# Output projection of the last stage on two steps at once, in one written order

## The chip, the core and the metric

The kernel runs on one core of a Trainium2 chip. The metric is the time of one execution on the device in microseconds, median of a few runs. Five engines work side by side, each through its own queue of instructions in order: TensorE (PE, its weight loads shown apart as PEld), VectorE (DVE), ScalarE (ACT), GpSimd (POOL) and SyncE (SP), which here only issues transfers. An engine waits for another only where an instruction carries a wait.

## The reference

The inputs are x (2048 tokens of 640 numbers), weights in fp32, 32 heads of 20 numbers each. Two branches are computed and mixed by a gate per token:

```
g   = sigmoid(x . gate_w)
q, k, v = x @ wqkv, per head
phi(t) = [softmax(t @ w_phi), softmax(-(t @ w_phi))]        # 40 numbers a head
kv  = sum over tokens of phi(k)^T v ;  z = sum of phi(k)
o   = (phi(q) @ kv) / (phi(q) . z + 1e-6)
a   = o @ wo
b   = silu(x @ w1) @ w2
out = g * a + (1 - g) * b
```

## The kernel before

Everything is kept transposed on the chip: features on the 128 partitions, tokens along the free side. Nearly every product is made from a high part and a low part of each number (fp32r each), in three passes: high x high, high x low, low x high (`PASSES`). The keys and values come first, then branch b, whose result, already multiplied by 1 - g, is written to a buffer in device memory (`fb_d`). The last stage makes branch a for the 2048 tokens and adds `fb_d` to it. The change concerns only this stage.

The last stage goes by steps u = 0 to 7 of 256 tokens, that is two q tiles of 128 tokens each. The tiles of steps 0 and 1 are finished before it; those of steps 2 to 7 are numbered 0 to 11 here (`QT`), tiles 2u - 4 and 2u - 3 for step u. A q tile goes through this chain:

- projection (pq, `q_proj`, line 542): 30 matmuls of 320 columns on TensorE, from a split x (`xb_load`, `xb_split`: a transfer, a cast on ScalarE, a difference on POOL);
- spikes (`q_max`, `q_sub`, lines 526 to 533): maximum and minimum per head, and two differences, on VectorE;
- exponential (`q_exp`, line 1192) on ScalarE;
- sum (`q_sum`, line 1196) on VectorE, and beside it the product with z (`q_norm`, ez, line 1209) on POOL, whose sum (`q_norm_sum`, line 1212) is again VectorE's;
- small sums (`q_small`: lines 1223 to 1239) on VectorE, which give each head's factor, and its product with the exponentials (`q_mul`, line 1245) on POOL.

A step u then is:

- transposes (pT, `t_mm`, line 1480): six of them on TensorE, each copied out of PSUM by ScalarE to fT (`t_out`, line 1496);
- the heads' products (pn, `n_mm`, line 1587), in three parts; ScalarE casts each part's high half to oT (`n_hi`, lines 1600 to 1603) and VectorE makes the low half, the remainder (`n_lo`, lines 1608 and 1610);
- output projection (pa, `w_mm`, line 1629): for each of five blocks of 128 output features 16 matmuls of 256 columns: five chunks in each of the three passes, and a rest. The first ten need only high halves of oT, the next five the low halves, and the last the rest. Two blocks share one PSUM bank (groups 0, 2, with 32 matmuls), the fifth has its own (group 4, with 16).

Then the sum: in steps 0 to 4 ScalarE copies the group out of PSUM (`w_copy`, line 1641) and POOL adds it to y, which a transfer brought from `fb_d` (`w_add`, line 1647); in steps 5 to 7 VectorE adds it straight out of PSUM. A transfer stores y.

PSUM banks: projections of q have two pairs of banks (`pair`). All other tiles of this stage, pT, pn and pa, take four single banks in turn (`single`), so each tile waits until the tile four calls before has been read. 

What sets the order: within the stage the queues of TensorE, VectorE, ScalarE and POOL keep the order in which the functions are called (`inorder`); SyncE's order is set by a scheduler. `step(u)` runs the transposes of step u, the output projection of step u - 1, two projections, and the heads' products of step u, interleaved by hand; `last_steps` writes out the end.

Of the kernel before, what the change touches and what calls it, by code (L numbers as in the profile page):

```python
# [16 lines left out]
P = 128  # L17
# [32 lines left out]
PAB = 2  # L50
# [78 lines left out]
NSEV = 4  # L129
ORDERS = (HEAD, O1, O2, O3, O4, O5, O6, O7, O8, O9, O10)  # L130
# [4 lines left out]
def mix_kernel(ctx: ExitStack, tc: tile.TileContext, xT, wqT, wkc, wkr, wv, bd, bdc, cst, wo, w1, w1r, w2, out):  # L135
# [1439 lines left out]

    def n_mm(u, gp, a):
        if (gp, a) == (0, 0):
            oTs[u] = tb.tile([P, 2, NG + 1, 256], F32R, tag="oT", name=f"oT{u}", bufs=2)
# [16 lines left out]
    pns = {}  # L1595

    def n_hi(u, gp):
        o, pn = oTs[u], pns[u, gp]
        if gp < 2:
            nc.scalar.copy(o[:, 0, 2 * gp : 2 * gp + 2, :], pn)  # L1600
        else:
            nc.scalar.copy(o[:, 0, 4, :], pn[:, 0])
            nc.scalar.activation(o[:GW, 1, 5, :], pn[:GW, 1], AF.Copy, scale=stk[:GW, 0:1])

    def n_lo(u, gp):
        o, pn = oTs[u], pns.pop((u, gp))
        k = slice(2 * gp, 2 * gp + 2) if gp < 2 else slice(4, 5)
        nc.vector.tensor_tensor(o[:, 1, k, :], pn[:, : k.stop - k.start], o[:, 0, k, :].bitcast(F32), op=ALU.subtract)  # L1608
        if gp == 2:
            nc.vector.scalar_tensor_tensor(  # L1610
                o[:GW, 0, 5, :], pn[:GW, 1], stk[:GW, 1:2], o[:GW, 1, 5, :].bitcast(F32), op0=ALU.mult, op1=ALU.add
            )

    ws = {}

    def w_mm(u, m0, n):
        o = oTs[u]
        if m0 == 2:
            y = fu.tile([P, 512], F32, tag="ur", name=f"y{u}_{m0}", bufs=2).rearrange("p (a s) -> p a s", a=2)
        else:  # L1620
            y = tb.tile([P, 2, 256], F32, tag="y", name=f"y{u}_{m0}", bufs=2)
        cols = slice(PB[u] * 256, (PB[u] + 1) * 256)
        nc.sync.dma_start(y[:, :n], fb_d[m0 : m0 + n, :, cols].rearrange("m p s -> p m s"))
        pa = single(f"pa{u}_{m0}").rearrange("p (a s) -> p a s", a=2)
        todo = [(c, ho, hw) for ho, hw in PASSES for c in range(NG)] + [(NG, 0, 0)]
        for a in range(n):
            ds = slice((m0 + a) * P, (m0 + a + 1) * P)
            for k, (c, ho, hw) in enumerate(todo):
                nc.tensor.matmul(  # L1629
                    pa[:, a, :],  # L1630
                    wo_tile[0][:, c, hw, ds] if c < NG else WOR[:, ds],
                    o[:, ho, c, :] if c < NG else o[:GW, ho, c, :],
                    start=(k == 0),
                    stop=(k == len(todo) - 1),
                )
        ws[u, m0] = y, pa, n, cols

    def w_copy(u, m0):
        y, pa, n, cols = ws[u, m0]
        a = tb.tile([P, 2, 256], F32, tag="pa", name=f"pac{u}_{m0}", bufs=PAB)[:, :n]  # L1640
        nc.scalar.copy(a, pa[:, :n])
        ws[u, m0] = y, a, n, cols

    def w_add(u, m0):
        y, pa, n, cols = ws.pop((u, m0))
        eng = nc.vector if pa.space == PSUM else nc.gpsimd
        eng.tensor_tensor(y[:, :n], pa[:, :n], y[:, :n], op=ALU.add)
        nc.sync.dma_start(out[m0 * P : (m0 + n) * P, cols].rearrange("(m p) s -> p m s", p=P), y[:, :n])

    def on(t, *todo):  # L1650

        if 0 <= t < len(QT):
            for part in todo:
                part(QT[t])

    def q_mm(t):
        q_open(t, q_proj(t))

    def x_next(k):
        for p in range(xb_done[0], min(xb_done[0] + k, len(XP))):  # L1660
            xb_split(p)
            x_ahead(p + 4)
            xb_done[0] = p + 1

    def x_ahead(p):
        if p < len(XP):
            xb_load(p)

    xb_done = [3]
    for p in range(3, 5):  # L1670
        x_ahead(p)

    def t_all(u, first, last):
        for i in range(first, last):
            t_mm(u, i)
            t_out(u, i)

    def n_all(u):
        for gp in range(3):
            for a in range(2):  # L1680
                n_mm(u, gp, a)
            n_hi(u, gp)

    def spikes(t):
        on(t, q_max, lambda t: q_sub(t, 0), lambda t: q_sub(t, 1), q_exp)

    def step(u):
        a, b, c = 2 * u - 2, 2 * u - 1, 2 * u
        x_next(3)
        t_all(u, 0, 4)  # L1690
        on(b, q_mm)
        on(a, q_norm_sum)
        t_all(u, 4, 6)
        spikes(b)
        on(a, q_small)
        on(b, q_norm)
        on(a, q_mul)
        w_mm(u - 1, 0, 2)
        w_copy(u - 1, 0)
        w_add(u - 1, 0)  # L1700
# [132 lines left out]
```

## Time and profile before

| | |
|---|---|
| median of 3 runs | 730.0 us (729.78 to 730.61) |
| the profiled execution | 730.17 us |
| its span in the trace | 728.4 us |
| TensorE busy, matmuls / weight loads | 721.2 us / 621.0 us |
| VectorE, ScalarE, POOL busy | 429.9, 297.4, 395.6 us |

The span is what lies between the first and the last instruction; the execution takes a little more. A row of a group of instructions gives line, engine, operation, what is written from what, shape and count, then busy time, mean ns of one, and the idle time of the engine just ahead of them with what ended it. A row of the chain gives start, length, engine, tile, line and number of instructions merged. A row of the order of time has start and length in us and ends with the idle time ahead in brackets. Matmuls run into one another, so the spacing of a run of them, its length divided by its number, is their price, not the duration of one.

### The profile page before, as it was taken

How to read it: one execution, taken by the hardware profiler on the slowest of the kernel's cores; microseconds unless marked ns; L12 is line 12 of the kernel's file. 1: busy time of each engine (PE TensorE's matmuls, PEld its weight loads, DVE VectorE, ACT ScalarE, POOL GpSimd, SP SyncE). 2: the span in 40 equal slices, each digit the busy share in tenths (PEclk: the TensorE clock that was granted, in tenths of full speed). 3: DMA queues.
4: the chain of work that ended last, by engine and by line, in shares of the span. 5: the costliest groups of instructions: out<-in, count | busy, mean ns of one | idle time of the engine just before them, and what ended most of it. 6: DMA issues, size and time to landing. Idle time of an engine off the chain costs nothing.

```text
span 728.4 us, 12513 instructions
## 1 busy us (share of the span) xinstructions
PE 721.2 (99%) x4935; PEld 621.0 (85%) x4935; DVE 429.9 (59%) x708; ACT 297.4 (41%) x558; POOL 395.6 (54%) x307
## 2 busy tenths in 40 slices
PE   9999999999999999999999999999999999999998
PEld 8888888888888888888888788788997899999988
DVE  4565555565253557568525656653887766766652
ACT  5333322336466354435344323535334453435330
POOL 2354545534756475572766447311598867767440
PEclk9999999999999999999999999999999999999999
DMA  8111111114734577588965623342133332121222
GB/s 306 56 56 56 46 56 55 63 35 135 238 116 176 213 276 277 207 314 324 330 205 188 219 68 107 109 117 73 52 115 119 102 95 83 56 94 45 74 87 81
DMA packets 50751, 98.80 MB, mean 136 GB/s; under 512 B 6352, under 2 KB 25828, under 8 KB 50692
## 3 DMA queue, kind: packets, MB, share of 16 engines
q1 hardware_dynamic: 50692, 98.00, 40.0%
q8 instruction: 39, 0.64, 0.4%
q14 instruction: 20, 0.16, 0.1%
HBM read 66.15 MB, written 31.84 MB: 135 GB/s over the span
## 4 chain that ended last, share of the span: by engine, by line
PE 97%; DVE 1%; ACT 1%; DMA 1%; issue 0%; DVEq 0%; ACTq 0%
PE o L1053 18%; PE kvp L566 17%; PE pa L1629 10%; PE pq L542 9%; PE a L964 9%; PE o L1094 5%; PE ph L632 3%; PE c L964 3%; PE b L964 3%; PE d L964 3%; PE pn L1587 3%; PE pT L1480 2%; PE hp L651 2%; PE kvt L553 2%; PE o_m L1116 1%; PE kvp L440 1%
## 5 line engine op out<-in xcount | busy, mean ns | idle before, releaser
L1053 PE MATMUL o<-u,w 128*128 128x512 f32 x580 | 142.5, 391 | 0.0
L1053 PEld LDWEIGHTS o<-u,w 128*128 128x128 f32 x580 | 108.0, 188 | 22.7 <-DVE acc L1058 0.6
L566 PE MATMUL kvp<-wh,xa 128*128 128x480 f32 (+2 forms) x420 | 92.5, 360 | 0.0
L566 PEld LDWEIGHTS kvp<-wh,xa 128*128 128x128 f32 x420 | 72.8, 188 | 10.4
L1629 PE MATMUL pa<-oT,wo 128*128 128x256 f32 x600 | 77.1, 281 | 0.1
L363 POOL TENSOR_TENSOR w<-wr,w 128x640 fp32r<-128x640 f32 x26 | 41.8, 1615 | 64.5 <-ACT w L352 64.5
L1629 PEld LDWEIGHTS pa<-oT,wo 128*128 128x128 f32 x600 | 73.8, 188 | 1.1 <-DVE oT L1608 0.8
L1209 POOL TENSOR_TENSOR ez<-eq,zbc 128x1280 f32<-128x1280 f32 x16 | 48.0, 3002 | 47.6 <-DVE sm L1239 24.6
L594 POOL TENSOR_TENSOR ek<-ek,st 128x1280 f32<-128x1280 f32 x16 | 38.2, 2386 | 50.3 <-DVE st L593 42.1
L542 PE MATMUL pq<-wq,xb 128*128 128x320 f32 x360 | 55.9, 312 | 0.0
L542 PEld LDWEIGHTS pq<-wq,xb 128*128 128x128 f32 x360 | 52.9, 188 | 2.2 <-DVE oT L1608 2.0
L1058 DVE TENSOR_TENSOR acc<-acc,o 128x512 f32<-128x512 f32 x70 | 46.4, 679 | 14.2 <-PE o L1053 14.1
L978 ACT ACTIVATE v<-v 128x512 f32<-128x512 f32 x33 | 20.9, 632 | 82.9 <-DVE v L997 36.2
L194 POOL TENSOR_TENSOR xa<-xra,xa 128x512 fp32r<-128x512 f32 (+1 forms) x26 | 26.4, 1038 | 41.4 <-ACT xa L192 37.0
L566 PE MATMUL kvp<-wl,xa 128*128 128x480 f32 (+2 forms) x210 | 47.6, 356 | 0.0
L1192 ACT ACTIVATE eq<-eq 128x1280 f32<-128x1280 f32 x16 | 20.4, 1276 | 63.9 <-DVE eq L533 63.9
L980 DVE TENSOR_TENSOR u<-v,u 128x512 fp32r<-128x512 f32 x29 | 21.5, 742 | 34.4 <-ACT u L979 31.5
L399 ACT COPY v<-kvp 128x340 f32<-128x340 f32 (+1 forms) x30 | 12.5, 417 | 70.1 <-PE kvp L566 68.2
L566 PEld LDWEIGHTS kvp<-wl,xa 128*128 128x128 f32 x210 | 36.6, 188 | 4.8
L1084 DVE TENSOR_TENSOR acc<-acc,o 128x512 f32<-128x512 f32 x48 | 31.3, 682 | 15.6 <-PE o L1094 12.1
L1245 POOL TENSOR_TENSOR eq<-eq,sm 128x1280 f32<-128x1280 f32 x16 | 37.9, 2368 | 1.0 <-DVE sm L1239 0.8
L592 DVE TENSOR_REDUCE st<-ek 128x64 f32<-128x1280 f32 x16 | 23.8, 1487 | 22.7 <-ACT ek L728 21.3
(236 smaller groups left out, 1483.7 us busy)
## 6 DMA issues: line engine op xcount, KB each, us to landing
wr<-w SPq DMA_DIRECT2D x33, 320.0 KB
w_d<-w SPq DMA_DIRECT2D x15, 640.0 KB
xr<-xT SPq DMA_DIRECT2D x27, 256.0 KB
w<-w_d SPq DMA_DIRECT2D x10, 640.0 KB
fb_d<-acc SPq DMA_DIRECT2D x20, 256.0 KB
s_d<-s SPq DMA_DIRECT2D x8, 512.0 KB
sa<-s_d SPq DMA_DIRECT2D x8, 512.0 KB
y<-fb_d SPq DMA_DIRECT2D x16, 256.0 KB
```

The costliest lines, as they stand in the source:

```text
L363: eng.tensor_tensor(t[:, 1, :], r[:, :D], t[:, 0, :].bitcast(F32), op=ALU.subtract)
L542: nc.tensor.matmul(dst, xt[c][:, hx, :], w[:, c, hw, lo : lo + n], start=first, stop=(hx == 1 and c == NC - 1))
L566: nc.tensor.matmul(kv_cols(t, lo, hi), xt[c][:, hx, :], WKV[hw][:, c, w_cols(lo, hi)], start=(n == 0), stop=(n == 3 * NC - 1), skip_group_ ...
L594: nc.gpsimd.tensor_tensor(groups(e), groups(e), spread(st[:, 1, :]), op=ALU.mult)
L964: last["mm"] = nc.tensor.matmul(out, lhs, rhs, start=(first and i == 0), stop=(stop and i == len(todo) - 1), skip_group_check=True)
L1053: nc.tensor.matmul(o, lhs, rhs, start=(n == 0), stop=(n == len(todo) - 1))
L1058: nc.vector.tensor_tensor(acc[j][m], acc[j][m], o, op=ALU.add)
L1084: nc.vector.tensor_tensor(acc[j][m], acc[j][m], o, op=ALU.add)
L1094: nc.tensor.matmul(o, ws[hw], x()[hx], start=(first and i == 0), stop=(i == len(PASSES) - 1), skip_group_check=True)
L1209: nc.gpsimd.tensor_tensor(ez, Q[t]["e"], zbc, op=ALU.mult)
L1245: nc.gpsimd.tensor_tensor(groups(q["e"]), groups(q["e"]), spread(q["sm"][:, 2 * H : 4 * H]), op=ALU.mult)
L1629: nc.tensor.matmul(pa[:, a, :], wo_tile[0][:, c, hw, ds] if c < NG else WOR[:, ds], o[:, ho, c, :] if c < NG else o[:GW, ho, c, :], start= ...
```

## The change

Steps are put together in groups p for the output projection: (0, 1), (2, 3), (4, 5), 6 and 7. For the three pairs oT holds 512 columns, the two steps side by side, the rest has a tile of its own (oR, with its high half in oM), and each of the five blocks is one PSUM bank, 16 matmuls of 512 columns. Steps 6 and 7 keep 256 columns. `w_mm` can be called in two halves. All adds are VectorE's, out of PSUM; the copies to `pac` and their buffers are gone. The helper functions of the order (`step`, `last_steps` and others) are replaced by one list of names, `FIN`, of which this is the beginning:

```diff
-PAB = 2
+FIN = """
+t04 f04 t05 f05 q0p R n000 n001 h00 n010 n011 h01 n020 n021 h02 x5l x6l q0m l00 l01 l02 q0s0 q0s1 t10
...
+    OUT = ((0, 1), (2, 3), (4, 5), (6,), (7,))
...
     def n_mm(u, gp, a):
         if (gp, a) == (0, 0):
-            oTs[u] = tb.tile([P, 2, NG + 1, 256], F32R, tag="oT", name=f"oT{u}", bufs=2)
+            p = max(u // 2, u - 3)
+            k = OUT[p].index(u)
+            if k == 0:
+                oTs[p] = (
+                    tb.tile([P, 2, NG, 512], F32R, tag="oT", name=f"oT{p}", bufs=2),
+                    tb.tile([P, 512], F32R, tag="oR", name=f"oR{p}", bufs=2),
+                )
+            cols = slice(k * 256, (k + 1) * 256)
+            mids[u] = oTs[p][0][:, :, :, cols], oTs[p][1][:GW, cols]
...
+    def w_parts(p, m0):
+        n = 1 if p < 3 else min(2, NC - m0)
+        return n, 256 * len(OUT[p]), PB[OUT[p][0]] * 256
+
+    def w_mm(p, m0, k):
+        o, rest = oTs[p]
+        n, size, at = w_parts(p, m0)
+        if k == 0:
+            pool, tag = (fu, "ur") if m0 // (1 if p < 3 else 2) % 2 else (tb, "y")
+            y = pool.tile([P, 512], F32, tag=tag, name=f"y{p}_{m0}", bufs=2)[:, : n * size]
+            y = y.rearrange("p (a s) -> p a s", a=n)
+            nc.sync.dma_start(y, fb_d[m0 : m0 + n, :, at : at + size].rearrange("m p s -> p m s"))
+            ws[p, m0] = y, single(f"pa{p}_{m0}")[:, : n * size].rearrange("p (a s) -> p a s", a=n)
+        pa = ws[p, m0][1]
+        todo = [(a, i) for a in range(n) for i in range(len(TERMS))]
+        half = len(todo) // 2
+        for a, i in todo[half * k : half * (k + 1)]:
+            c, ho, hw = TERMS[i]
             ds = slice((m0 + a) * P, (m0 + a + 1) * P)
...
+            nc.tensor.matmul(
+                pa[:, a, :],
+                wo_tile[0][:, c, hw, ds] if c < NG else WOR[:, ds],
+                o[:, ho, c, :size] if c < NG else rest[:GW, :size],
+                start=(i == 0),
+                stop=(i == len(TERMS) - 1),
+            )
...
-    def w_copy(u, m0):
-        y, pa, n, cols = ws[u, m0]
-        a = tb.tile([P, 2, 256], F32, tag="pa", name=f"pac{u}_{m0}", bufs=PAB)[:, :n]
-        nc.scalar.copy(a, pa[:, :n])
-        ws[u, m0] = y, a, n, cols
...
+    def w_add(p, m0):
+        y, pa = ws.pop((p, m0))
+        n, size, at = w_parts(p, m0)
+        nc.vector.tensor_tensor(y, pa, y, op=ALU.add)
+        nc.sync.dma_start(out[m0 * P : (m0 + n) * P, at : at + size].rearrange("(m p) s -> p m s", p=P), y)
...
+        for name in FIN.split():
+            ops.pop(name)()
```

Three places show how instructions move. In the rows a number after a name is the step (pT, fT, pn), the group (oT, pa, y) and its block, or the tile (pq, eq); x15 means fifteen alike in a row.

The entry of the stage, ScalarE. eq0 is the exponential of tile 0, xb_1 are the casts of the next x, fT1 the copies of step 1's transposes. Before:

```order
L1603 ACTIVATE oT0_5337<-pn0_2_5350,stk_89 120x256
L1192 ACTIVATE eq0_5333<-eq0_5333 128x1280
L192 CAST xb_1_0_5373<-xrb_1_0_5285 128x512
L192 CAST xb_1_2_5378<-xrb_1_2_5287 128x512
L192 CAST xb_1_4_5383<-xrb_1_4_5357 128x256
L1496 COPY fT1_0_5393<-pT1_0_5388 120x512
L1496 COPY fT1_0_5393<-pT1_1_5395 120x512
```

and now:

```order
L1633 ACTIVATE oM0_5356<-pn0_2_5351,stk_89 120x256
L1516 COPY fT1_0_5376<-pT1_0_5371 120x512
L1516 COPY fT1_0_5376<-pT1_1_5378 120x512
L1516 COPY fT1_2_5389<-pT1_2_5384 120x512
L1516 COPY fT1_2_5389<-pT1_3_5391 120x512
L1212 ACTIVATE eq0_5333<-eq0_5333 128x1280
L1516 COPY fT1_4_5405<-pT1_4_5400 120x512
L1516 COPY fT1_4_5405<-pT1_5_5407 80x256
```

The copies stand ahead of the exponential; the casts of x moved behind the heads' products of step 1.

Step 3, TensorE, from the heads' products on. Before:

```order
L1587 MATMUL pn3_1_6070<-fT3_2_5956,kvw_4607 64x256 x4
L1587 MATMUL pn3_2_6076<-fT3_4_6004,kvw_4607 64x256 x2
L1587 MATMUL pn3_2_6076<-fT3_4_6004,kvwr_4608 64x256
L1587 MATMUL pn3_2_6076<-fT3_4_6004,kvwr_4608 56x256
L542 MATMUL pq6_6091<-wq_4604,xb_3_0_5923 128x320 x2
L542 MATMUL pq6_6091<-wq_4604,xb_3_2_5928 128x320 x2
```

and now:

```order
L1618 MATMUL pn3_1_5927<-fT3_2_5898,kvw_4607 64x256 x4
L1618 MATMUL pn3_2_5933<-fT3_4_5911,kvw_4607 64x256 x2
L1618 MATMUL pn3_2_5933<-fT3_4_5911,kvwr_4608 64x256
L1618 MATMUL pn3_2_5933<-fT3_4_5911,kvwr_4608 56x256
L1665 MATMUL pa1_0_5957<-oT1_5713,wo_4668 128x512 x15
L1665 MATMUL pa1_0_5957<-oR1_5714,wor_s_5280 128x512
L562 MATMUL pq6_5983<-wq_4604,xb_3_0_5830 128x320 x2
```

Where a projection stood behind the heads' products, a group that reads their result stands now. The same place on VectorE, before:

```order
L1608 TENSOR_TENSOR oT3_6063<-pn3_0_6064,oT3_6063 128x512
L1212 TENSOR_REDUCE sm5_5995<-ez5_6020 128x64
L1223 SCALAR_TENSOR_TENSOR sm5_5995<-pq5_5964,sm5_5995 128x32
L1224 TENSOR_TENSOR sm5_5995<-sm5_5995,pq5_5964 128x64
L1229 TENSOR_REDUCE sm5_5995<-sm5_5995 128x32
L1230 RECIPROCAL sm5_5995<-sm5_5995 128x32
L1239 SCALAR_TENSOR_TENSOR sm5_5995<-pq5_5964,g_87,sm5_5995 128x64
L526 TENSOR_REDUCE mmq6_6123<-pq6_6091 128x32
L527 TENSOR_REDUCE mmq6_6123<-pq6_6091 128x32
L533 TENSOR_TENSOR eq6_6124<-pq6_6091,mmq6_6123 128x32x20
L533 TENSOR_TENSOR eq6_6124<-mmq6_6123,pq6_6091 128x32x20
L1608 TENSOR_TENSOR oT3_6063<-pn3_1_6070,oT3_6063 128x512
```

and now:

```order
L553 TENSOR_TENSOR eq5_5878<-pq5_5845,mmq5_5877 128x32x20
L553 TENSOR_TENSOR eq5_5878<-mmq5_5877,pq5_5845 128x32x20
L1243 SCALAR_TENSOR_TENSOR sm4_5798<-pq4_5767,sm4_5798 128x32
L1244 TENSOR_TENSOR sm4_5798<-sm4_5798,pq4_5767 128x64
L1249 TENSOR_REDUCE sm4_5798<-sm4_5798 128x32
L1250 RECIPROCAL sm4_5798<-sm4_5798 128x32
L1259 SCALAR_TENSOR_TENSOR sm4_5798<-pq4_5767,g_87,sm4_5798 128x64
L1638 TENSOR_TENSOR oT1_5713<-pn3_0_5921,oT1_5713 128x2x256
L1638 TENSOR_TENSOR oT1_5713<-pn3_1_5927,oT1_5713 128x2x256
L1638 TENSOR_TENSOR oT1_5713<-pn3_2_5933,oT1_5713 128x256
L1640 SCALAR_TENSOR_TENSOR oR1_5714<-pn3_2_5933,stk_89,oM3_5938 120x256
```

The three remainders stand together behind the spikes of tile 5 and the small sums of tile 4, where two of them stood behind a later tile's spikes.

Near the end, TensorE behind the heads' products of step 6. Before:

```order
L1587 MATMUL pn6_2_6876<-fT6_4_6806,kvwr_4608 56x256
L1629 MATMUL pa5_2_6896<-oT5_6605,wo_4668 128x256 x15
L1629 MATMUL pa5_2_6896<-oT5_6605,wor_s_5280 128x256
...
L1629 MATMUL pa5_4_6933<-oT5_6605,wo_4668 128x256 x15
L1629 MATMUL pa5_4_6933<-oT5_6605,wor_s_5280 128x256
L1480 MATMUL pT7_0_6952<-ident_81,eq10_6666 120x128 x2
```

and now:

```order
L1618 MATMUL pn6_2_6614<-fT6_4_6580,kvwr_4608 56x256
L1665 MATMUL pa2_3_6635<-oT2_6166,wo_4668 128x512 x15
L1665 MATMUL pa2_3_6635<-oR2_6167,wor_s_5280 128x512
L1665 MATMUL pa2_4_6656<-oT2_6166,wo_4668 128x512 x15
L1665 MATMUL pa2_4_6656<-oR2_6167,wor_s_5280 128x512
L1665 MATMUL pa3_0_6677<-oT3_6600,wo_4668 128x256 x15
L1665 MATMUL pa3_0_6677<-oR3_6601,wor_s_5280 128x256
```

The first group of step 6 (pa3_0) stands ahead of step 7's transposes; it is the fourth single bank after pn6_1. On VectorE the remainder of pn6_1 stands, as before, behind the sum over ez11 and the small sums of tile 11.

More of the change, by code (lines that the diff above doesn't have):

```diff
@@ L1650, in on @@
[L1650 to L1676, printed above, removed]
```

166 lines of the change are left out of this document (56 added, 110 removed).

## The prediction

> **What bounds the kernel now.** The page's first part comes first, then the chain that ended last for the final stage, which the change rewrites.
>
> ```profile
> span 728.4 us, 12513 instructions
> PE 721.2 (99%) x4935; PEld 621.0 (85%) x4935; DVE 429.9 (59%) x708; ACT 297.4 (41%) x558; POOL 395.6 (54%) x307
> ```
>
> TensorE fills the span. The chain shows what a step of the last stage is made of (start, length, what, times):
>
> ```profile
> 617.53 3.79 PE pa L1629 x32
> 621.32 2.74 PE pn L1587 x24
> 624.06 4.59 PE pq L542 x30
> 628.66 5.68 PE pa L1629 x48
> 634.33 1.75 PE pT L1480 x16
> 636.08 4.41 PE pq L542 x30
> 640.49 0.66 PE pT L1480 x6
> 641.15 3.79 PE pa L1629 x32
> ...
> 725.08 0.42 DVE y L1647
> ```
>
> A step takes 641.15 - 617.53 = 23.62 us, all of it TensorE, and nothing but TensorE is on the chain until the last add. So the time falls by what is taken from TensorE and rises by each wait put before it. The stretches show how near the others are (duration, then busy time of PE, PEld, DVE, ACT, POOL):
>
> ```profile
> 552.00:564.00 12.00, 10.98 (x84) 9.07 (x83) 8.26 (x13) 4.14 (x9) 10.04 (x10) 1.00 0.37 133
> 564.00:576.00 12.00, 11.19 (x86) 9.82 (x86) 8.80 (x13) 7.79 (x13) 7.99 (x5) 1.00 0.45 141
> 612.00:636.00 24.00, 24.00 (x192) 22.73 (x191) 16.45 (x26) 10.44 (x20) 17.32 (x12) 1.00 0.26 83
> ```
>
> In the steady part VectorE is busy 16.45 of 24 us, and the clock is full (1.00). Only the entry, 552 to 576, has holes. TensorE's own waits there:
>
> ```profile
> PEld pT L1480 <- POOL eq L1245: 1.2, 1, 1.2
> PEld pT L1480 <- ACT fT L1496: 1.0, 1, 1.0
> PEld pa L1629 <- ACT fT L1496: 0.3, 1, 0.3
> ```
>
> I take the weight loads' waits (PEld), since the load is what a matmul starts with; the matmul rows look busy through their modelled ends.
>
> **Term 1, the matmuls: -2.4 us.** Steps 0 to 5 use 480 matmuls of 256 columns (six steps of 80); now 240 of 512 columns do the same. The row above gives 3.79 / 32 = 118.4 ns for 256 columns. For 512 columns of the same kind the earlier chain has
>
> ```profile
> 303.24 4.08 PE o L1053 x18
> ```
>
> which is 226.7 ns. A pair becomes 226.7 instead of 236.8: 10.1 ns, times 240 is 2.4 us. The other end is 236.8, no gain, if the price goes with the columns; I take 226.7, as it is measured on the same size. The Trainium skill (TensorE: Matmul & The Clock Gate, "Back-to-back issue gap") speaks against so much: its isolated gap, columns / 2.4 + 2.5 ns, is an estimate of 109.2 and 215.8 ns, 2.6 ns per pair and 0.6 us in all. The trace does not agree with its 109.2, for it has 118.4.
>
> **Term 2, the entry: -1.3 us.** How the two waits of the entry on ScalarE come about:
>
> ```profile
> 559.76 2.36 POOL L1245 TENSOR_TENSOR eq<-eq,sm 128x1280 f32<-128x1280 f32 x1
> 562.17 1.50 PEld L1480 LDWEIGHTS pT<-ident,eq 128*120 128x120 f32 x14 [1.24 <-POOL eq L1245]
> 563.10 0.81 DVE L533 TENSOR_TENSOR eq<-mmq,pq 128x640 f32<-128x640 f32 x1
> 568.13 0.41 ACT L192 CAST xb<-xrb 128x256 fp32r<-128x256 f32 x1 [1.88 <-DMA xrb<-xT]
> 568.44 2.78 ACT L1496 COPY fT<-pT 120x512 f32<-120x512 f32 x6
> 569.07 0.65 PEld L1480 LDWEIGHTS pT<-ident,eq 128*120 128x120 f32 x6 [1.01 <-ACT fT L1496]
> 570.04 1.83 PEld L1629 LDWEIGHTS pa<-oT,wo 128*128 128x128 f32 x15 [0.33 <-ACT fT L1496]
> ```
>
> The quoted rows are POOL's product, the transposes behind it, the last spike of tile 0 (ends 563.91), the casts, the copies and what waits for them. The casts of x stand ahead of step 1's copies in ScalarE's queue, and the last waits for its transfer until 568.09. Now those copies stand ahead of the casts, so 1.01 + 0.33 go. The 1.24 on POOL's product of the exponentials (ends 562.12) stays: what makes it is not touched. The casts wait for the same transfer, whose load stands behind three loads of y on SyncE as it stood behind four, but they are wanted only by projection 2, after two groups of the output projection; ScalarE takes them some 6 us after 568.09.
>
> **Term 3, the adds: nothing by themselves.** Fifteen POOL adds and fifteen ScalarE copies go:
>
> ```profile
> L1647 POOL TENSOR_TENSOR y<-pac,y 128x512 f32<-128x512 f32 x10 | 13.0, 1302 | 0.0
> L1641 ACT COPY pac<-pa 128x512 f32<-128x512 f32 x10 | 5.8, 576 | 0.8 <-PE pa L1629 0.7
> L1647 DVE TENSOR_TENSOR y<-pa,y 128x512 f32<-128x512 f32 x6 | 4.1, 688 | 14.6 <-PE pa L1629 14.6
> ```
>
> Neither engine holds the chain, so their relief is worth nothing directly. VectorE takes five adds per two steps, 5 x 0.69 = 3.4 us more in 47, beside 33: about 78% busy. It is covered by TensorE unless TensorE waits for what stands behind an add. The loads of y and x and the stores keep SyncE's queue: a store waits for its add, and loads stand behind it. Each pair's four y buffers come free a whole group cycle (tens of us) ahead of need, so no transfer enters the sum. Stores and loads are as many bytes. The end (final groups, last add of 0.42, last store) is word for word the same work: 0.
>
> **Term 4, new waits: +1.9 us.** Before, each step's projection group was issued a step later, behind work of its own; now the first group of a pair follows at once on the heads' matmuls (n) of its second step, and needs n's VectorE remainders (L1608, L1610) at its 11th, 13th, 15th and 16th matmul. What VectorE does per q tile, to lay along the new order:
>
> ```profile
> 616.91 0.82 DVE L526 TENSOR_REDUCE mmq<-pq 128x32 f32<-128x640 f32 x1 [2.98 <-PE pq L542]
> 619.85 0.18 DVE L1223 SCALAR_TENSOR_TENSOR sm<-pq,sm 128x32 f32<-128x32 f32 x1
> 621.27 1.50 DVE L1196 TENSOR_REDUCE pq<-eq 128x64 f32<-128x1280 f32 x1
> 624.26 1.49 DVE L1212 TENSOR_REDUCE sm<-ez 128x64 f32<-128x1280 f32 x1 [0.57 <-POOL ez L1209]
> 625.78 0.19 DVE L1223 SCALAR_TENSOR_TENSOR sm<-pq,sm 128x32 f32<-128x32 f32 x1
> 631.63 1.01 DVE L1608 TENSOR_TENSOR oT<-pn,oT 128x512 fp32r<-128x512 f32 x2
> 632.56 0.47 DVE L1610 SCALAR_TENSOR_TENSOR oT<-pn,stk,oT 120x256 fp32r<-120x256 f32 x1
> 633.05 1.50 DVE L1196 TENSOR_REDUCE pq<-eq 128x64 f32<-128x1280 f32 x1
> 631.74 1.28 ACT L1192 ACTIVATE eq<-eq 128x1280 f32<-128x1280 f32 x1 [6.88 <-DVE eq L533]
> 633.10 2.93 POOL L1209 TENSOR_TENSOR ez<-eq,zbc 128x1280 f32<-128x1280 f32 x1 [2.96 <-ACT eq L1192]
> ```
>
> The first row starts 0.03 us after its projection's last matmul, and one engine's end to the next one's start is 0.03 (VectorE, ScalarE) to 0.08 (POOL) all along, as from 631.74 + 1.28 to 633.10. Spikes (L526 to L533): 619.85 - 616.91 = 2.94. Small sums (L1223 to L1239): 621.27 - 619.85 = 1.42. Exponential 1.28, its product on POOL 2.93, a sum 1.5, remainders 633.05 - 631.63 = 1.42 for two of three, about 2.0 for all.
> - Step 1 (pair 0). Copies come first on ScalarE, so the exponential of tile 0 runs about 564.6 to 565.9, POOL's product to 568.9, VectorE's sum to 570.4, spikes of tile 1 to 573.3, remainders 574.0, 574.6, 575.4. TensorE, without its waits, is through n at 571.6; its 16th matmul is due at 571.6 + 15 x 0.227 = 575.0. Wait 0.65.
> - Step 2. Transposes 2 and 3 take the banks of the second and third projection group, which VectorE's adds must empty. They stand behind the spikes of tile 2, and these behind the sums of tile 1, whose product on POOL now follows the x splits. Laid out: sums of tile 1 to 584.4, add, spikes to 588.0, add ends 588.7; TensorE ends the first group at 575.9 and has two more (3.63 each), a projection (4.5) and two of the six transposes (0.88) before it: 588.5. Waits 0.25 and 0.2.
> - Steps 3 and 5 (pairs 1, 2). From the end of the projection of tile 4 (in pair 1) VectorE needs 0.8 (tile 3's small sums, two remainders and an add are still ahead of it), spikes, one add 0.65, exponential, product, sum, spikes, small sums, remainders: 0.8 + 2.94 + 1.4 + 3.0 + 1.5 + 2.94 + 1.42 + 2.0 = 16.0, some 16.2 with hand-overs (the add runs beside the exponential). TensorE has one group 3.63, projection 4.5, transposes 2.41, n 2.74 and 15 matmuls 3.4: 16.68. Spare about 0.5, so only ScalarE's last cast shows, under 0.1 each.
> - Step 6. The group after pair 2 takes the bank of n's second part, whose remainder stands behind the sums of tile 11: 2.94 + 1.28 + 2.93 + 1.5 + 1.42 + 0.69 = 10.8 plus some hand-overs, against transposes, n and two groups, 0.66 + 2.74 + 7.26 = 10.66. Wait 0.55.
>
> With 0.2 for the casts: 0.65 + 0.45 + 0.55 + 0.2 = 1.9. From below it is 0, if all is covered; from above the dearest wait shown, 1.24, at the four places (steps 1, 3, 5, 6) and the 0.45: 5.4.
>
> **Sum.** -2.4 - 1.3 + 0 + 1.9 = -1.8 us. The profiled execution took 730.17 (728.4 span, 1.8 around it), which gives 728.4; its time lies 0.17 above the median, so from 730.0 I predict 728.2.
>
> **Rivals.** (a) VectorE becomes the bound at the pair's joint, slower: steps 3 and 5 have only some 0.5 us to spare, and the 24 us stretch above shows VectorE with 16.45 us of work, which grows. If its work there comes more than 0.5 us later than laid out, each joint waits; this decides from 1.8 us of waits in all beyond the 1.9 (at 3.7 nothing is won), and at 1.24 for each of the four it gives -3.7 + 5.4 = +1.7, 731.7. Against it: the rows' sequence is regular and POOL has less to do. (b) The wide matmul brings nothing: 236.8 per pair leaves -1.3 + 1.9 = +0.6, 730.6; the measured 226.7 speaks against it. By the skill's estimate above it would be 730.0. (c) All new waits are covered: -3.7, 726.3; against it, step 1's and step 6's queues don't fit by the rows.
>
> **How the numbers follow.** The forecast, 728.2 within some 1.2 us, has 0.53; a measurement of this kernel tells 0.2%, 1.5 us, from no change, so faster starts at 728.5, and I give 0.36 of it to faster and 0.17 to same. (a) has 0.18, of which 0.16 is slower, 0.02 same; (b) 0.16, same; (c) 0.13, faster. So faster 0.49, same 0.35, slower 0.16. The range from 726.3 to 731.8 reaches (c) and (a) and leaves out about 0.15. The forecast's own range is 727.0 to 729.4.
>
> **What would show it.** Right: matmuls of 128x512 at about 227 ns in the chain, steps of 23.2 us; the 1.0 wait on the copies gone from the entry; waits of TensorE for VectorE's remainders or adds in steps 1, 2 and 6 of 0.2 to 0.7 each, none over 0.2 in 3 and 5. Wrong: those waits repeat in every pair or exceed 1 us (a), or the chain shows over 232 ns per wide matmul (b).

## The result, and the profile after

The changed kernel takes 728.46 us (median of 11 runs, 728.09 to 729.38) beside 730.02 of the kernel before: a ratio of 0.9977, 95% interval 0.9968 to 0.9985. That is 1.6 us less, where 728.2 us was predicted. The sum came out by luck: two of its terms were each wrong by about 1 us, in opposite directions.

The page's first part, for the changed kernel (its profiled span beside 728.4 us before):

```profile
span 726.5 us, 12020 instructions
PE 719.8 (99%) x4695; PEld 608.4 (84%) x4695; DVE 435.8 (60%) x720; ACT 288.9 (40%) x543; POOL 380.1 (52%) x292
```

The chain of the changed kernel in the last stage (start, length, what, times):

```profile
605.93 3.68 PE pa L1665 x16
...
619.16 3.89 PE pa L1665 x16
623.05 4.40 PE pq L562 x30
627.45 7.38 PE pa L1665 x32
634.83 1.75 PE pT L1500 x16
...
723.29 0.42 DVE y L1676
```

Sixteen wide matmuls take 3.68 us, 230 ns each, and 32 take 7.38, 230.6 ns: dearer than the 226.7 ns that the prediction took from an earlier stage. The waits of TensorE's weight loads in the order of time, in the brackets with what ended them:

```profile
562.23 2.14 PEld L1500 LDWEIGHTS pT<-ident,eq 128*120 128x120 f32 x20 [1.24 <-POOL eq L1265]
...
571.70 2.14 PEld L1665 LDWEIGHTS pa<-oT,wo 128*128 128x128 f32 x10 [0.39 <-ACT oT L1629]
574.07 0.30 PEld L1665 LDWEIGHTS pa<-oT,wo 128*128 128x128 f32 x2 [0.23 <-DVE oT L1638]
574.66 0.53 PEld L1665 LDWEIGHTS pa<-oT,wo 128*128 128x128 f32 x3 [0.30 <-DVE oT L1638]
575.39 0.19 PEld L1665 LDWEIGHTS pa<-oR,wor_s 120*128 120x128 f32 x1 [0.19 <-DVE oR L1640]
...
588.66 0.95 PEld L1500 LDWEIGHTS pT<-ident,eq 128*120 128x120 f32 x8 [0.36 <-PE pT L1500]
588.69 1.16 PE L1500 MATMUL pT<-ident,eq 128*120 128x128 f32 x8 [0.15 <-DVE y L1676]
...
698.77 1.83 PEld L1665 LDWEIGHTS pa<-oT,wo 128*128 128x128 f32 x15 [0.53 <-DVE oT L1638]
```

The waits of 1.01 and 0.33 on ScalarE's copies at the entry are gone, the 1.24 on POOL stays. New waits stand in step 1 (0.23, 0.30, 0.19), step 2 (0.36) and step 6 (0.53), and none on VectorE in steps 3 and 5. (The load of step 2 names TensorE in its bracket; the matmul it belongs to, the row behind it, names VectorE's add, L1676. The 0.39 behind the heads' products stood before as well, ahead of whatever followed them.) The stretches (duration, then busy time of PE, PEld, DVE, ACT, POOL) show the entry filled, and VectorE with 17.29 us in place of 16.45 in the steady part:

```profile
564.00:576.00 12.00, 12.00 (x78) 9.50 (x77) 8.50 (x15) 7.13 (x13) 3.67 (x2) 1.00 0.24 80
612.00:636.00 24.00, 24.00 (x151) 20.58 (x150) 17.29 (x30) 9.22 (x18) 16.59 (x9) 1.00 0.25 81
```

**How the runs are compared.** The last stage begins anywhere from 558.0 to 559.2 us in the profiled executions, also where nothing ahead of it was edited. So I measure the stage itself: from the start of its first heads' matmul to the start of its last matmul. Of the kernel before, in the order of time:

```profile
558.00 1.92 PEld L1587 LDWEIGHTS pn<-fT,kvw 120*64 120x64 f32 x20 [0.19 <-issue]
...
724.76 0.28 PE L1629 MATMUL pa<-oT,wor_s 120*128 120x256 f32 x1
```

and of the changed one:

```profile
558.05 1.92 PEld L1618 LDWEIGHTS pn<-fT,kvw 120*64 120x64 f32 x20 [0.19 <-issue]
...
722.97 0.28 PE L1665 MATMUL pa<-oR,wor_s 120*128 120x256 f32 x1
```

166.76 and 164.92 us: the change is worth 1.84 us by this measure. Each length is that of one execution. Two experiments below whose edits turn out to move nothing (e7 and e10) give 164.99 and 164.91, so it repeats within 0.1 us, and the sums here are made with it. The medians of whole executions, with intervals of about 0.1% to either side, agree in direction, but several of them overlap.

| kernel | median, us | ratio to before (95% interval) | stage, start to end | its length |
|---|---|---|---|---|
| before | 730.0 to 730.6 | 1 | 558.00 to 724.76 | 166.76 |
| after | 728.46 | 0.9977 (0.9968 to 0.9985) | 558.05 to 722.97 | 164.92 |
| e1_narrow | 729.38 | 0.9986 (0.9977 to 0.9995) | 558.89 to 724.71 | 165.82 |
| e2_entry_old | 727.93 | 0.9969 (0.9958 to 0.9980) | 559.23 to 723.47 | 164.24 |
| e3_before_late_casts | 729.20 | 0.9985 (0.9976 to 0.9994) | 558.98 to 724.40 | 165.42 |
| e4_waits_gone | 727.61 | 0.9960 (0.9948 to 0.9973) | 558.42 to 722.36 | 163.94 |
| e5_adds_pool | 732.15 | 1.0023 (1.0013 to 1.0032) | 558.24 to 727.42 | 169.18 |
| e6_vector_late | 729.75 | 0.9989 (0.9979 to 0.9999) | 558.59 to 724.72 | 166.13 |
| e7_two_banks | 728.50 | 0.9976 (0.9965 to 0.9987) | 558.26 to 723.25 | 164.99 |
| e8_narrow_no_waits | 728.75 | 0.9975 (0.9965 to 0.9986) | 558.19 to 723.43 | 165.24 |
| e9_adds_pool_two_copies | 746.26 | 1.0217 (1.0200 to 1.0234) | 558.23 to 739.02 | 180.79 |
| e10_operands | 728.17 (one run) | | 558.01 to 722.92 | 164.91 |
| e11_no_wait_left | 727.80 | 0.9971 (0.9960 to 0.9982) | 558.21 to 722.55 | 164.34 |
| e12_entry_old_step6 | 727.33 | 0.9960 (0.9946 to 0.9973) | 558.19 to 722.08 | 163.89 |

### The profile page after: what moved, and what is told of

Its sections match the earlier page's. It is cut to its first block, busy times and chain, and to the rows that moved or that the text cites. A ratio compares the mean times of both kernels' runs of the same rounds, so it can differ in the third digit from the quotient of the medians.

```text
span 726.5 us, 12020 instructions
## 1 busy us (share of the span) xinstructions
PE 719.8 (99%) x4695; PEld 608.4 (84%) x4695; DVE 435.8 (60%) x720; ACT 288.9 (40%) x543; POOL 380.1 (52%) x292
## 4 chain that ended last, share of the span: by engine, by line
PE 78%; POOL 7%; issue 7%; DVE 6%; ACT 1%; DMA 0%; SPq 0%; POOLq 0%; DVEq 0%; ACTq 0%
PE kvp L586 17%; PE o L1073 14%; PE a L984 9%; PE pa L1665 5%; PE o L1114 5%; POOL ez L1229 4%; PE pq L562 3%; PE ph L652 3%; PE c L984 3%; PE b L984 3%; PE d L984 3%; PE hp L671 2%; PE kvt L573 2%; PE o_m L1136 1%; PE kvp L460 1%
## 5 line engine op out<-in xcount | busy, mean ns | idle before, releaser
L1665 PE MATMUL pa<-oT,wo 128*128 128x512 f32 (+1 forms) x375 | 74.2, 350 | 0.1
L1665 PEld LDWEIGHTS pa<-oT,wo 128*128 128x128 f32 x375 | 59.8, 188 | 12.2 <-issue 1.6
```

The costliest lines, as they stand in the source:

```text
L1665: nc.tensor.matmul(pa[:, a, :], wo_tile[0][:, c, hw, ds] if c < NG else WOR[:, ds], o[:, ho, c, :size] if c < NG else rest[:GW, :size], st ...
```

## The experiments

In the names of `FIN` a first digit is the step or pair. t and f are transposes and their copies, n the heads' products, h their casts, l the remainders, w and d a group and its add. x3l is a load of x, x3s its cast and split. After q and the tile's number, p is the projection, m s0 s1 the spikes, e the exponential, S and Z the two sums, z the product ez, P i k the small sums, M the last product.

### The new waits: e4_waits_gone

```diff
-q1m q1s0 q1s1 n100 n101 h10 n110 n111 h11 n120 n121 h12 q1e x3s x7l x4s x8l x5s x9l l10 l11 l12
+q1m n100 n101 h10 n110 n111 h11 n120 n121 h12 x3s x7l x4s x8l x5s x9l l10 l11 l12 q1s0 q1s1 q1e
...
-l60 q11Z q11P q11i q11k q11M l61 l62
+l60 l61 l62 q11Z q11P q11i q11k q11M
```

> The changed kernel, with two moves in VectorE's order: step 1's three remainders ahead of the subtractions of tile 1's spikes, and the last two remainders of step 6 ahead of the sums of tile 11. Theory (the new waits come from these places in VectorE's queue and from nothing else): the waits of 0.72 (step 1) and 0.53 (step 6) go, the one of step 2 (0.36) is at most as long; 1.2 to 1.6 us faster than after, 726.9 to 727.3. Rival (what is pushed back, the spikes of tile 1 and the small sums of tile 11, is late in its turn, and the waits only move): within 0.4 of after, 728.1 to 728.8.

All three new waits went, step 2's too, and none came in their place. But the stage became only 0.98 us shorter, not 1.2 to 1.6. The weight loads of step 1 in the order of time show why; first of the changed kernel, from its first wide group to the projection behind the second:

```profile
571.70 2.14 PEld L1665 LDWEIGHTS pa<-oT,wo 128*128 128x128 f32 x10 [0.39 <-ACT oT L1629]
...
579.18 4.52 PEld L562 LDWEIGHTS pq<-wq,xb 128*128 128x128 f32 x30
```

then of this kernel:

```profile
572.07 3.28 PEld L1664 LDWEIGHTS pa<-oT,wo 128*128 128x128 f32 x15 [0.39 <-ACT oT L1628]
...
579.30 4.54 PEld L561 LDWEIGHTS pq<-wq,xb 128*128 128x128 f32 x30
```

The two groups take 579.18 - 571.70 = 7.48 us with the waits and 579.30 - 572.07 = 7.23 without: the brackets add up to 0.72, the loss is 0.25. Step 6's wait cost 0.37 (of 0.53): by the starts of the matmuls its groups take 11.629 us, here 11.254. A bracket counts the time in which the weight load stood idle; these loads run under the wide matmul before them, which goes on for another 0.23 us, so up to that much of each wait is covered. (The Trainium skill, Perfetto Trace Analysis, "Tensor Engine Instruction (MATMUL, LD_WEIGHTS)", states that weight loads can be pulled ahead of matmuls under way; these rows agree with it.) Step 2's wait stands among short transposes, and there nothing was covered: its 16 transposes take 2.104 us, here 1.667, a loss of 0.44, more than the bracket of 0.36. The three losses are 1.06 in all, of which 0.98 shows in the stage.

### The width: e1_narrow and e8_narrow_no_waits

e1 is the changed kernel with each wide group issued as two runs of 256 columns; e8 is the same edit on e4, where no wait can hide the difference.

```diff
-        todo = [(a, i) for a in range(n) for i in range(len(TERMS))]
+        parts = [(a, slice(j, j + 256)) for a in range(n) for j in range(0, size, 256)]
+        todo = [(*part, i) for part in parts for i in range(len(TERMS))]
...
-                pa[:, a, :],
+                pa[:, a, j],
```

> The changed kernel, with each group of 16 matmuls of 512 columns issued as 16 of 256 for the first step's columns and then 16 of 256 for the second's; order, adds and everything else stay. Theory (the wide matmul saves what the trace of after shows, about 3.79 - 3.60 to 3.72 = 0.07 to 0.19 us per group, 15 groups, 1.1 to 2.8, and the waits of steps 1, 2 and 6 shrink a little because TensorE comes later): 1 to 2.3 us slower than after, about 729.5 to 730.8, groups of 3.79 us in the trace. Rival (the order alone makes the gain, the width brings nothing): as after, 728.3 to 728.6.

> The kernel of e4_waits_gone with each wide group as two runs of 256 columns as in e1_narrow: no wait is left that could hide the difference. From the first heads' matmul to the last matmul e4_waits_gone takes 163.94 us. Theory (a wide matmul in this stage takes 230 ns, the pair of narrow ones 236.8: 6.5 ns times 240 is 1.6 us): 165.5. The prediction's 226.7 ns would give 10.1 ns times 240 = 2.4 us: 166.3. Rival (width brings nothing): 163.9 to 164.2.

e1 is 0.90 us longer than after: less than the 1.0 to 2.3 expected, because the waits shrank under the longer matmuls. None is left on a weight load in steps 1 and 6, and step 2's bracket is 0.28. e8 settles it: 165.24 beside 163.94, so the width is worth 1.30 us where no wait hides it, less than the 1.6 and the 2.4 of e8's theory. Divided by 240 it is 5.4 ns per pair. The chains of e8 and of e4 in pair 1 (start, length, what, times):

```profile
605.76 3.78 PE pa L1665 x32
...
619.09 3.97 PE pa L1665 x32
...
627.45 7.57 PE pa L1665 x64
```

```profile
605.63 3.68 PE pa L1664 x16
...
618.86 3.88 PE pa L1664 x16
...
627.14 7.37 PE pa L1664 x32
```

0.10, 0.09 and 0.20 us for one, one and two groups. The Trainium skill's isolated gap (TensorE: Matmul & The Clock Gate, "Back-to-back issue gap") gave an estimate of 0.6 us; the same section's figure for a stream, 131 ns at 512 columns, does not fit the 230 ns here either.

### Why 230 ns and not 226.7: e7_two_banks and e10_operands

```diff
+        if p in (1, 2) and m0 in (1, 2):
+            todo = [(ws[p, m][1], m, 0, i) for i in range(len(TERMS)) for m in (1, 2)] if (m0, k) == (2, 1) else []
...
-q6p w11a w11b q6m q6s0 q6s1 q6e d11 w12a w12b d12
+q6p w11a w11b w12a w12b q6m q6s0 q6s1 q6e d11 d12
```

> The changed kernel, with the matmuls of the second and third wide group of pairs 1 and 2 issued in turn, one into the one PSUM bank, the next into the other, 32 matmuls in all. In after these 32 take 7.38 us from the first of them to what follows (230.6 ns each), while the earlier stage's wide matmuls take 226.7. Theory 1 (the 3.9 ns are the price of 16 sums in a row into the same bank): 7.25 us. Theory 2 (they belong to the operands, the weights or what runs beside): 7.38 us as before. VectorE's adds come later, so transposes of the next step may wait by up to 0.7 us; only the length of the 32 tells the theories apart.

```diff
+            cw, cx = (0 if p == 1 else c), (0 if p == 2 else c)
+            if c < NG and p in (1, 2):
+                ho, hw = (0 if p == 2 else ho), (0 if p == 1 else hw)
...
-                wo_tile[0][:, c, hw, ds] if c < NG else WOR[:, ds],
-                o[:, ho, c, :size] if c < NG else rest[:GW, :size],
+                wo_tile[0][:, cw, hw, ds] if c < NG else WOR[:, ds],
+                o[:, ho, cx, :size] if c < NG else rest[:GW, :size],
```

> The changed kernel; in pair 1 all wide matmuls but the last of each group take the same weights (chunk 0, high part), in pair 2 all but the last take the same moving rows (chunk 0, high part). So the outputs of these pairs are other sums, and waits on remainders go in pair 2; the work of a matmul is the same. After has 7.38 us for 32 wide matmuls in both pairs (230.6 ns), the earlier stage 226.7 ns. If fetching the changing weights is what costs the 3.9 ns: 7.25 us in pair 1, 7.38 in pair 2. If the changing moving rows cost it: 7.38 and 7.25. If neither: 7.38 in both.

The 32 matmuls of e7 in the chain:

```profile
627.67 7.36 PE pa L1667 x32
```

those of e10 in pair 1 in the chain, and in pair 2 in the matmuls' order of time (starts 673.96 and 681.33, 7.37 apart):

```profile
627.39 7.38 PE pa L1668 x32
```

```profile
673.96 3.61 PE L1668 MATMUL pa<-oT,wo 128*128 128x512 f32 x15
...
681.33 1.91 PE L1500 MATMUL pT<-ident,eq 128*120 128x128 f32 x16
```

Neither the bank, nor the changing weights, nor the changing moving rows make the 3.9 ns. The granted clock (the share of the full clock that TensorE gets) is 1.00 in the stretch. The starts of the single matmuls in after's trace split the price: inside a group they are 226, 229 and 232 ns apart in turn, 229 in the mean, and 226 or 227 in the earlier stage. The other 1.3 to 1.6 ns per matmul lie at the two ends of a group, where four distances are 233 to 238 ns; the last matmul there is the rest's, of another shape, which both experiments keep. Why the inner ones are 2.3 ns dearer is open; what the other engines do beside was not varied.

### The entry: e3, e2 and e12

e3 is the kernel before with the x casts of step 1 behind that step's copies, and nothing else:

```diff
         a, b, c = 2 * u - 2, 2 * u - 1, 2 * u
-        x_next(3)
+        if u > 1:
+            x_next(3)
         t_all(u, 0, 4)
...
         t_all(u, 4, 6)
+        if u == 1:
+            x_next(3)
```

> The kernel before, with one thing moved: the three x casts and splits of step 1 stand behind that step's copies of the transposes instead of ahead of them. Theory (the entry's waits come from this place in ScalarE's queue alone): the waits of 1.0 and 0.3 go and nothing takes their place, since the first group of before is step 0's, whose remainders are long done: 1.2 us faster than before, about 728.8. Rival (something else, POOL's splits or the next projection, holds the same place): a new wait of about 1 us, 729.8 to 730.2.

The stage is 1.34 us shorter than before, and both waits are gone, as the last transposes of step 1 show in the order of time (1.01 in brackets before):

```profile
569.01 0.70 PEld L1480 LDWEIGHTS pT<-ident,eq 128*120 128x120 f32 x6
```

So the term of 1.3 us has its size, and moving the casts behind the copies in ScalarE's queue suffices for it. e2 does the reverse: the changed kernel with before's order at the entry.

```diff
-q0m l00 l01 l02 q0s0 q0s1 t10 f10 t11 f11 t12 f12 t13 f13 q0e q0z t14 f14 t15 f15 q0S q1p
-q0Z q1m q1s0 q1s1 n100 n101 h10 n110 n111 h11 n120 n121 h12 q1e x3s x7l x4s x8l x5s x9l l10 l11 l12
+q0m l00 l01 l02 q0s0 q0s1 q0e q0z q0S x3s x7l x4s x8l x5s x9l t10 f10 t11 f11 t12 f12 t13 f13 q1p
+q0Z t14 f14 t15 f15 q1m q1s0 q1s1 n100 n101 h10 n110 n111 h11 n120 n121 h12 q1e l10 l11 l12
```

> The changed kernel, with the order of before up to the transposes of step 1: x casts ahead of step 1's copies, projection of tile 1 ahead of the last transposes. Theory A (the terms add up): the waits of 1.0 and 0.3 on the copies come back and nothing else moves, 1.3 us slower than after, 729.8. Theory B (entry and the waits of steps 1 and 2 hang together: VectorE's pace from tile 0's exponentials on is the same, so TensorE that comes 1.1 us later finds remainders and adds ready): the two waits on the copies come back, the waits of step 1 (0.72) and step 2 (0.36) go, and the time is within 0.4 of after, 728.3 to 728.9.

Both theories missed: the stage is 0.68 us shorter than after. The waits of steps 1 and 2 went as B said (tile 1's projection, and so its spikes, come earlier), but the waits on the copies did not come back. That could have been the chance of an execution whose stage began late, so e12 takes the same entry with step 6's move from e4:

> The kernel of e2_entry_old, with the last two remainders of step 6 ahead of the sums of tile 11 as in e4_waits_gone. e2_entry_old took 164.24 us from the first heads' matmul to the last matmul, without a wait of TensorE on ScalarE's copies at the entry, and e4_waits_gone 163.94. Theory (with the order of FIN the third x tile lands early enough whatever the execution, so x casts ahead of step 1's copies cost nothing, and the step 6 wait costs 0.37): 163.9, about 727.4. Rival (e2 was spared only because its last stage began 1.2 us later in that execution, 559.23 against 558.05): the waits of 1.0 and 0.3 are back, 164.5 to 165.2.

163.89 us with the stage's start at 558.19, close to before's 558.00: no chance. The cast that waits for the third part of x, in e12:

```profile
567.19 0.41 ACT L211 CAST xb<-xrb 128x256 fp32r<-128x256 f32 x1 [0.74 <-DMA xrb<-xT]
```

9.00 us after the stage's start, where before has it at 568.13, 10.13 after. SyncE's queue, before and in e12:

```profile
561.78 1.91 SPq L1623 DMA_DIRECT2D y<-fb_d  x4
563.74 8.11 SPq L285 DMA_DIRECT2D xrb<-xT  x5
```

```profile
556.08 0.32 SPq L1656 DMA_DIRECT2D y<-fb_d  x1
...
562.04 1.27 SPq L1656 DMA_DIRECT2D y<-fb_d  x3
563.36 8.65 SPq L304 DMA_DIRECT2D xrb<-xT  x5
```

One of four loads of y now goes out 6 us earlier, so the loads of x start 5.17 us after the stage's start instead of 5.74. That is half of the 1.13; the rest is in the transfer, and was not taken apart. By its median e12 is the fastest kernel of the study, 727.33 us; by its ratio, 0.9960 (0.9946 to 0.9973), it is level with e4.

### VectorE's spare at the joints: e6_vector_late

A joint is the place where a pair's first group follows the heads' products of its second step.

```diff
-        nc.vector.tensor_tensor(o[:, 1, k, :], pn[:, : k.stop - k.start], o[:, 0, k, :].bitcast(F32), op=ALU.subtract)
+        for _ in range({(3, 0): 2, (5, 0): 4}.get((u, gp), 1)):
+            nc.vector.tensor_tensor(o[:, 1, k, :], pn[:, : k.stop - k.start], o[:, 0, k, :].bitcast(F32), op=ALU.subtract)
```

> The changed kernel, with work added to VectorE alone ahead of the joints: the first remainder of step 3 is computed twice (0.62 us more), that of step 5 four times (1.85 us more); the values stay. Prediction's own sizes (spare of 0.5 us at each joint): about 0.1 us at step 3 and 1.3 at step 5 appear as TensorE's time. By the trace of after (last remainder of step 5 ends 668.19, its load starts 669.15, spare about 1.0): 0 at step 3, 0.9 at step 5. Rival (the joint is already on VectorE, no spare): 0.6 at step 3 and 1.85 at step 5.

Step 3 took as long as in after (25.21 us from its heads' products to step 4's, in both). In step 5 TensorE lost 1.19 us, 26.39 against 25.20. VectorE's remainders and the load that waits for them, each in the order of time:

```profile
666.79 3.79 DVE L1639 TENSOR_TENSOR oT<-pn,oT 128x512 fp32r<-128x512 f32 x6
```

```profile
669.70 0.30 PEld L1666 LDWEIGHTS pa<-oT,wo 128*128 128x128 f32 x2 [1.16 <-DVE oT L1639]
```

Of the changed kernel, the remainders at the same place:

```profile
666.19 1.61 DVE L1638 TENSOR_TENSOR oT<-pn,oT 128x512 fp32r<-128x512 f32 x3
```

The six remainders take 3.79 us where after's three take 1.61, so 2.18 were added (a repeat costs 0.73, not the 0.62 expected), and 2.18 - 1.19 = 1.0 us is the spare: what after's trace said, twice the prediction's 0.5.

### The adds on POOL: e5 and e9

```diff
-        nc.vector.tensor_tensor(y, pa, y, op=ALU.add)
+        eng = nc.vector
+        if p < 3:
+            eng, a = nc.gpsimd, tb.tile([P, 512], F32, tag="pa", name=f"pac{p}_{m0}", bufs=1)
+            nc.scalar.copy(a, pa[:, 0])
+            pa = a.rearrange("p (a s) -> p a s", a=1)
+        eng.tensor_tensor(y, pa, y, op=ALU.add)
...
-            mids[u] += (tb.tile([P, 256], F32R, tag="oM", name=f"oM{u}", bufs=2)[:GW],)
+            mids[u] += (tb.tile([P, 256], F32R, tag="oM", name=f"oM{u}", bufs=1)[:GW],)
```

The second edit, one buffer for the rest's high half, makes room.

> The changed kernel, with the 15 adds of the wide groups as they were before: ScalarE copies the sums out of PSUM, POOL adds (one buffer for the copy). Measured from the first heads' matmul of step 0 to the last matmul, after takes 164.92 us. Theory (the adds are nothing by themselves, but VectorE's place for them makes step 2's wait): the wait of step 2 on VectorE's add goes, nothing else changes, 164.5 to 164.9. Rival 1 (taking POOL and ScalarE out was itself a gain, since their queues hold the x splits and the exponentials' products): 165.5 or more, with waits on POOL or ScalarE in the trace. Rival 2 (VectorE's five adds per pair cost at the joints): 164.2 or less.

4.26 us slower: rival 1, and more than it said. 3.51 us of it fall into step 2 (from its predecessor's heads' products to its own 29.38 us, in after 25.87), and 0.24, 0.30 and 0.17 into steps 3, 5 and 6. Step 2's transposes wait for ScalarE's copies, in the order of time:

```profile
589.38 0.41 PEld L1500 LDWEIGHTS pT<-ident,eq 128*120 128x120 f32 x4 [0.89 <-ACT pac L1679]
591.34 0.46 PEld L1500 LDWEIGHTS pT<-ident,eq 128*120 128x120 f32 x4 [1.55 <-ACT pac L1679]
```

The first copy stands behind tile 2's exponential, the second also waits for POOL's add before it, since there is one buffer. Then the projection takes 5.73 us in the chain instead of 4.41, and the stretches show that the clock (third number from the end) was halved behind the waits:

```profile
592.22 5.73 PE pq L562 x30
```

```profile
590.00:592.00 2.00, 0.69 (x6) 0.66 (x5) 0.39 (x1) 1.29 (x3) 1.30 (x2) 0.91 0.17 44
592.00:594.00 2.00, 2.00 (x10) 2.00 (x9) 0.00 (x0) 2.00 (x6) 2.00 (x2) 0.50 0.85 293
594.00:596.00 2.00, 2.00 (x12) 2.00 (x11) 0.43 (x1) 0.59 (x2) 2.00 (x2) 0.73 0.45 157
```

So at least 1.3 us of the 4.26 are the clock's. e9 was to tell the queues from the single buffer:

```diff
-            eng, a = nc.gpsimd, tb.tile([P, 512], F32, tag="pa", name=f"pac{p}_{m0}", bufs=1)
+            eng, a = nc.gpsimd, tb.tile([P, 512], F32, tag="pa", name=f"pac{p}_{m0}", bufs=2)
...
-            y = pool.tile([P, 512], F32, tag=tag, name=f"y{p}_{m0}", bufs=2)[:, : n * size]
+            y = pool.tile([P, 512], F32, tag=tag, name=f"y{p}_{m0}", bufs=1 if pool is tb else 2)[:, : n * size]
```

> As e5_adds_pool, whose stage took 169.18 us from the first heads' matmul to the last matmul, 4.26 more than after, but with two buffers for ScalarE's copies, as before had them (one of the two buffers of y in the steps' pool is given up for the room). Theory 1 (the cost of e5 lies in the queues: in the new order POOL's x splits and products and ScalarE's casts stand ahead of adds and copies, so banks come free late and VectorE's chain at the joints is pushed back through POOL): most of it stays, 168 to 169.2. Theory 2 (it was the single copy buffer, a copy waiting for the add before it): 164.5 to 165.5.

It fits neither: giving up one buffer of y made adds wait for their loads. POOL's first such wait is 3.19 us long and ends at 593.86; VectorE's, at the end of the stage, are 20.0 us in three waits, 9.5 the longest:

```profile
DVE y L1681 <- DMA y<-fb_d: 20.0, 3, 9.5
```

Only step 2 says something, since TensorE's one wait in it (0.90, on the copy) is over at 589.36, before POOL's: 26.37 us, 0.50 more than after. So most of e5's 3.51 there is the single buffer and what it did to the clock. What POOL adds with all their buffers would cost in this order stays open; the 0.50 and e5's 0.24, 0.30 and 0.17 make an estimate of 1.2 us.

### The last wait: e11_no_wait_left

```diff
-to2 ig8 to3 ig9 qm15
+to2 qm15 ig8 to3 ig9
```

> The kernel of e4_waits_gone, with one more move, ahead of the last stage: POOL's product of the exponentials that step 1's transposes wait for (1.24 us) stands ahead of two products with the gates (2.5 us) instead of behind them. Theory (the wait goes, and TensorE then runs into VectorE's remainders of step 0 for about 0.5 us, since nothing speeds VectorE up): 0.7 us faster than e4_waits_gone, 163.2 us from the first heads' matmul to the last matmul, about 726.9. If nothing takes the wait's place: 162.7, 726.4. Rival (the gates' products are late in their turn, with the stores and loads of y behind them): 163.9 or more.

The rival: 0.40 us longer than e4. The wait on POOL went, and TensorE waited elsewhere; the load of step 1's transposes and, in VectorE's order of time, the rest of step 0:

```profile
563.91 1.05 PEld L1499 LDWEIGHTS pT<-ident,eq 128*120 128x120 f32 x10 [1.67 <-ACT fT L1515]
```

```profile
563.31 0.48 DVE L1639 SCALAR_TENSOR_TENSOR oR<-pn,stk,oM 120x256 fp32r<-120x256 f32 x1 [1.04 <-DMA fb_d<-acc]
```

By the trace the write of the rest waits for a store of branch b's result, which comes later now that the gate's product ahead of it does; it is the last reader of the bank that step 1's fourth transpose takes in turn, which starts at 563.91, 0.12 us after that write's end. (The bracket there names ScalarE's copies, which were done.)

## Why the prediction was right, and where it was wrong

Three differences of stage lengths make the change: before to e8, the new order without the new waits and without width, -1.52; e8 to e4, the width, -1.30; e4 to after, the waits, +0.98. Together -1.84, beside the prediction's -1.8. That the sums agree is luck: term 1 was 1.1 us too large, term 4 0.9, and the two errors cancelled. (The parts depend on their order, too: with the waits in place the width is worth 0.90, e1.)

- **Term 1, the matmuls (-2.4): mis-sized, -1.30 measured.** The mechanism holds, the step that failed is "I take 226.7, as it is measured on the same size". The row came from another stage; in this one a wide matmul takes 230 to 230.6 ns (e7 and e10 exclude three causes; the cause is open), which alone takes 240 x 3.3 to 3.9 ns = 0.8 to 0.9 us from the term. Another 0.1 is that 32 narrow ones take 3.78 us here, not 3.79. What is left, 0.1 to 0.2, is about what the rows resolve.
- **Term 2, the entry (-1.3): right in size, too simple in cause.** e3 has -1.34. But the step "stands behind three loads of y on SyncE as it stood behind four" was taken to change nothing, and e2 and e12 show that with the changed kernel's loads the casts would not have been late in their old place either. Either of two edits ends the wait. What the new entry order did beside that was to cost: 0.68 us against e2, in the waits of steps 1 and 2.
- **Term 3, the adds (0): right for the change as made**, since VectorE holds them without a wait in steps 3 and 5. That relief of POOL and ScalarE "is worth nothing directly" was not right of this order: e5 pays with them on POOL, though how much of it belongs to the adds is open.
- **Term 4, the waits (+1.9): mis-sized, +0.98 measured.** The places were right, and so were the brackets: predicted 0.65, 0.45, 0.55 in steps 1, 2, 6, found 0.72, 0.36, 0.53. What failed was to count such a bracket as lost time behind wide matmuls: 0.25 and 0.37 were lost in steps 1 and 6; step 2's 0.45 was right, 0.44. The layout's own figures gave less than was written, too: in step 1 575.4 - 575.0 = 0.4, not 0.65, and in step 6 10.8 - 10.66 = 0.1 and some hand-overs, not 0.55. VectorE's layout was good: the load of step 1's rest, laid out for 575.4, starts at 575.39. TensorE's was not quite, since without waits (e4) the 16th matmul starts 3.55 us behind the heads' products (575.62 - 572.07) and not 15 x 0.227 = 3.4. The 0.2 for the casts did not come.
- **Rivals.** (a) VectorE is not the bound at the joints: no wait there, and e6 finds 1.0 us to spare. The trigger "0.5 us" would have been 1.0. (b) The width does bring something: 1.30. (c) The covering of all waits is what e4 and e12 reach by hand; 163.9, 2.8 to 2.9 less than before, not the 3.7 the rival gave, for want of term 1's other half.
- **Signs.** "Matmuls at about 227 ns" were 230.6, below the 232 that was to speak for (b). Steps of 23.2 us: from pair 1's first group (619.09) to pair 2's (665.82) it is 46.73 us, 23.37 a step. The rest came as said.

The order's -1.52 beside e3's -1.34 leaves 0.18 us that no run took apart.

## What to carry to other kernels

A price from another stage is an estimate, even for the same shape: nearly half of term 1 was lost, most of it to 4 ns per matmul. A bracket ahead of a weight load is not the loss. Behind wide matmuls it was more (0.72 beside 0.25, 0.53 beside 0.37), since the load can run under the matmul before it; among short transposes it was less (0.36 beside 0.44). Compare the starts of what follows instead. And where a written order leaves an engine waiting for an add or a remainder, move that one item up in its engine's queue: two such moves (e4) gave another 0.98 us on top of the change's 1.84.

## What was not expected of the hardware

A wide matmul cost 1.5 to 1.7% more in this stage than in an earlier one at the same granted clock of 1.00, with the same shapes; the bank, the changing weights and the changing moving rows were excluded as causes. Inside the groups it is 229 ns beside 226.7, the rest lies at their ends.

Waits that come close together cost more than their length. In e5, 0.89 and 1.55 us of waiting within 2.9 us were followed by a projection of 5.73 us instead of 4.41. Single waits of 1.24 (entry) and 1.16 (e6) left the clock at 1.00. The trace has the times at which the granted clock changed, and in e5 and e9 each change behind such waits comes 3.41 us, or a multiple of it, after the one before. Stretches of 3.41 us cut along these times show what decided (TensorE's busy time comes first, the clock third from the end). In e5:

```profile
588.23:591.65 3.42, 1.47 (x12) 0.99 (x11) 1.50 (x1) 2.04 (x4) 1.70 (x3) 1.00 0.22 80
591.65:595.06 3.41, 3.41 (x16) 3.41 (x14) 0.00 (x0) 2.94 (x7) 3.41 (x2) 0.50 0.66 227
```

and in e9:

```profile
600.25:603.66 3.41, 1.94 (x9) 1.25 (x7) 3.27 (x9) 1.19 (x2) 0.96 (x2) 1.00 0.61 192
624.14:627.55 3.41, 1.22 (x5) 0.78 (x5) 3.27 (x10) 1.27 (x1) 1.74 (x1) 1.00 0.29 91
```

With 1.47 us of matmuls in one of these stretches, the next ran at half the clock; with 1.94 (and one wait of 2.06) it did not; with 1.22 it did, 627.55 to 630.97. So it is TensorE's work within such a stretch that counted in these three, not the length of one wait; where between 1.47 and 1.94 the line lies is not shown. The Trainium skill (TensorE: Matmul & The Clock Gate, "Part 1: The HAM clock gate") states that the clock is halved after an idle window of about 3.4 us; the 0.50 and the 3.41 agree, but here the window was not idle throughout.
